# Key and query products in two halves, and new order lists for all engines, in a gated mix of two attention layers

## The chip, the core and the metric

The kernel runs on one core of a Trainium2 chip. The time is the device time of one execution in microseconds (us). Before the change the median of three runs is 811.47 us (808.78 to 812.91).

## What is computed

Two attention layers run on the same input `x` (2048 rows of 512) and are mixed by a gate. `h` has 32 heads; layer A works in 64 segments of 32 rows, and each segment sees 8 memory rows, which are an output of the segment before it. That makes a chain of 64 links.

```python
g = _sigmoid((x * gate_w).sum(-1, keepdims=True))
return g * _A_ref(...) + (1 - g) * _B_ref(...)

# A: for each segment s of 32 rows
h = jnp.concatenate([mem, xs], axis=1)            # 8 + 32 rows
q, k, v = (jnp.einsum('btd,dhe->bhte', h, W) for W in (Wq, Wk, Wv))   # 32 heads of 128
p = _softmax(jnp.where(mask, jnp.einsum('bhqe,bhke->bhqk', q, k) * scale, -1e9))
o = jnp.einsum('bhte,hed->btd', jnp.einsum('bhqk,bhke->bhqe', p, v), Wo)
mem = o[:, :M, :]                                 # goes into the next segment
outs.append(o[:, M:, :])

# B: four blocks of 512 rows, 32 heads of 16: causal softmax inside a block, plus a
# linear-attention memory (phi(k)^T v) of the blocks before, mixed by sigmoid(beta), then wo
```

## The kernel before

**How the work is tiled.** For each segment of layer A TensorE (PE) makes the products of 32 rows (24 of the segment and the 8 memory rows, tile `hT`) with Wk, Wq and Wv. The 32 rows are the loaded weights, in four column groups of the array at once; the big matrices stream through in chunks of 512 columns. The contraction over 512 goes in four chunks. A product of one half of the heads (`r` is 0 or 1) has 4 chunks of 4 matmuls. `wproj` issues it. The products of the last 8 rows of each segment do not depend on the memory; they are made for four segments at a time (tile `xr`, names beginning with `r`, function `p_rest`), the value part goes out to memory (`rest_v`) and comes back (`rem_v`).

The names and lines used below:

- `k`, `q`, `v`: products of a segment, line 1466 (with a weight load) and line 124 (function `again`: the weights that are still in the array are used once more). The query product of the second half of the heads is made in two column halves of 256.
- copies out of PSUM by ACT or DVE: line 1040 (`st`, `V_sb`, `OT_sb`); transposes of keys and queries by DVE: line 1544.
- scores `S` (lines 1559, 1563), their exp on ACT (1568), sums `U` (1586, 124), logarithm and reciprocal on ACT (1589, 1591), normalisation on DVE (1593) and on DVE or GpSimd (1595).
- `PV` and `PW` (lines 1626, 1635): probabilities times values, row-tiled.
- output product `wo` (line 1352), turned by DVE (1370), swapped (1374) and added (1377): this gives the memory rows in `hT` for the next segment.
- layer B: logits (1184), exp (1202), mask on GpSimd (1208), values (1225), projections (1067, 1069); it fills the gaps of layer A. Changing between column-tiled, row-tiled and full use of the array is a change of mode.

**What sets the order.** Every operation is created once with its engine or a choice of engines, what it reads and writes, and a cost. The text `ORDER` holds, packed, one list of operation numbers for each of the five engines; `sequences` unpacks it, and `schedule` follows it (`given`). So the order on every engine, and the engine of each operation that has a choice, are what the text says. The planner's constants (`LATENCY`, `TO_PE`, the instruction packets of 256 in `fetched`) give each operation a time; with the order fixed, these times only choose PSUM banks and which waits are written out. 

**Weights that are held.** Operations of one `Share` may take their chunks in any order. `turn` walks along the TensorE order; an operation that directly follows one with the same key begins with the chunk whose weights are in the array, without a load:

```python
c = held[1] if held and held[0] == key and held[1] in left else left[0]
o.plan.append((c, held != (key, c), len(left) == o.share.total, len(left) == 1))
```

From segment 1 on, `k` and `q` products were one operation of four chunks, `v` products four operations of one chunk (argument `n` of `wproj`).

Of the kernel before, what the change touches and what calls it, by code (L numbers as in the profile page):

```python
# [15 lines left out]
    "c-nPY2Vhji)1STeF4uA?v>=^?&|5%yhY+L$k)VQrAcWpkgiu0n(u)*9k<bOC_Z~XZi6|=kK|vr1sdu@%x9^*MS6(^31g`Acot^TV-^^~-M`r8XMp|Ig6oFooTVNYGXX@;)^wVtFn%O{L-i3n@*B#C`"  # L16
    "cT8)`LDw(V+82JAtt+I@qaW7dJ+F6O<rWX!RP=Jz<srAqWx$1DtA>?2_3if0W`@qlw5DbQY`7VjYwVpKQ)%I}LVoT<LJ8;GqD_E^HxQonL(&U?D!)}Z7!SLWTI$>Y`$7ugVO=9QjPTkF@LQGo06jhD"
    "&Q3Ym!9(@~!1dJ0nwXEtthlv}Yv|lJp+VC#zq_F3L-=~*fA|>6Xh}2vQj3=*&viP~>T>O<pIcsQ05@`Mjp1%BfO83ln}0VFZl8rF=_!Q(99wdt9qcs~m_GUek_jPtx7o=#PoGH*b!d1EK+VT#Jz+=6"
    "%sy=PxfW~ztO2<4e)@5K?MQRBz1}H(c-0FQPazm_`ZIvaZa6aHwO=~g1P1FTL~G41=E~KYxJ&@EM+^5M&JDi;v?>5FdM6%*0+YQXuhp6z#<%u@Fjt-^a>GbBoc<ba0T{gV;LDw;Qpx5QU*TNdhC4y1"
    "tN9t6+H`(9H^jj_NR+m(p7wC5XFWhSo^uo5WIzSpz<bY1Km~Xnm<eTI;m)h59<L{8*i#(Hw_;S>`2btSFG@zwCG>thRTBM2_dVVBKy!Za1VSu0Y}Pq7kUQ!7{E_IQ<T({3)0(B=%euRwzF$s<5H2gE"  # L20
    "&;*OdgUJosf1fFt)((cPy4vtD3Cqztv=-g<xE!1dM(s6-Go5V$%bQ+=asK_MrlQ99Q|U3TCwg0ck=0pf*Fi3v=n;LlCcr%={xrl(;&%_hIKs`BBuxKW@7AFjXA<3c7Wlo~6M!0Sn9ss+O|lT-7XvrU"
    "e-kaQMGKq215}3K15@$}82&mE)=J*{14=b4Lj3$wt<YNRaadM}1_hgpo1i;bVACg(5~~;DO9hW3kDyqa1I+oMPQ-Q>OCId&3C@gIC@u#@e*Fs(Q+Ykw##Df$W7(XDOtfvSy^kcee!poeC-QpqvC#pG"
    "rs^C}xCmf=E}Owg)2jZ-c7KUbCzf@+0qoAgABO<$y%NT-c^q^&hBF?;K*`GMT0M@-vY8z?)$yR(vl`jYAR54}Gr+BSTVgYkVa;c#=$au+ZaIJ)Tj@+uf#$bd1WgFN6H^aiTkDU?4*^wyul>%NG#kD#"
    "o^1)R6Ya{zIOm`q4#&}MnmV_bU58-xF-haQ%`UV!2OXKlm>JW)h7d!xiD_)`>We=u&qA?R#Ts10k5<$mG|wwC8}sKkh(U?Fa>p)C4#Wy|g_wRD`YvYLipb3mojvZ`3Fy?RFd1USXa@FQ3k|Mq7#P=`"
    "C6M0u!7ki66oC%y(&znh78YIm_lg99Ut#hr_!v<@Y*Fw}6uf?8%{3K_TbpNb+4Egy*m{1egsu-^?!?cd+v^>AKC?;@v^&{$U%1=Tb{}HlTHZr+95}`fhL#c-j$s<)W$Yw`<8o}dwgRv>ypV6yusoWs"
    "`w}+&H$~EVJUHN|f!h#b=#94f?L`G)PLgNIv+?Fa-T<!TCGei4O5C=U(6CK|<88FzZyBZ3x?^`%hTFAYq8njv5^RS_|AWsq`^}6MU+oT}%`tOtN;}YTI`^kPYGDQ2*$wOTqb1pxRF#~w`G_3m>w_PF"
    "(Glttb7*a%9llSL(ZsRqaR8aq_=vnsy^FoJ^Lp;(xx`FU0Yo~?9w;<GKBF(6jR!gd4BrSkcPXt^^U{oT@mEQtplrsj%Nn<E!vZ)6kT6NkZ$7p#xg#?5T5$e2f)uVB6uMv}d0u)+3IkM{;Zwg0A5?=?"
    "Ee2}V!h>&ktw?Y!&Y5{bwi(e<8<4=|Nj3i~06vo;B*Il_DzN4vMpI$cFqrE{X}c3Rulaen1GjqAEA>pzbH-d<D9Hj_k?0IJ6kYp3bQ*#ge@cpiO^8rdH(tkJ-7t1N0MH3eyWw75$_>eFQz7ONq+{wu"
    "zIE7hb%^^LO~5Dg`%>NfYEGOBgIb=oL)I}~8=6Bb?HW#kFb5Ps<J(q0OZZ)NXx8R<v?esiR*28+XtY~*=p#2EjWr%C*<BtM<F_*8KZF_Qwm4X7WI$QK>^Rl=Ks+3QsAdun((u2bS6M>-tYpozpy0pj"
    "X2D;v@DOs}x45AYE^Ro(LL368+ThgVvnIn}eAi*(M`W@zg`3T_&blj_gQ+6YZw92LzLcaF2PiU>ex)tq%-NiAauoDKZHxvtEc<58$nFWlkl+rU1Xwi5r+Xx{#jiGAuXnpcfkD`#)jE%MGGC9)I6WHX"  # L30
    "#bePG4gL8;eEG%!+;{yBC+-W&vA;na?}GliOz?92vNd<$34@m8m??XQm&dnpFGVWQLACU77C<dj1^CMiuh?uUfUyHN0EE95IoVsG8Ns)|=!UHuZUCFd${Ax9=z{4}Ak}?LB)!X=uOsl{+x3#bM!OzV"
    "YsKpuU1T6*)M~<#pKZ^Ma>MSXRV1GchTSI<`G{<+L`Fx*hEI?&McgbJ1xw+<4oP5r#-{nanad_N5n(29!_5Y8wUryTMRk!R{!)~@i4J8Ptl@LD5SE1yX2t4pS#(j4-Ah+UKB~bg#^Cu)_h5Q;IV(;!"
    "=d+H-l-=xt3G$o5-;x5DwJ`RjuMUHKL+?UX0yuEgg@2^oBVfIAEUPJAyRlM&=fiz04?f2}=ZYk53N*w{XTRiehnO&R9=Tz|cu8K^k3CFA^bfjQH({aHp>yl9080H^2D`mLuGE|`cS2GHFGpDaC?4i4"
    "0LBppu(&|yof3lo!`Z^}e*@IM9p%2qYE?D69w3`VF&!cs9D+7D&$j>=ThxZKd#Ih}L3>K<SeAEmq2wp12>hVbsof6r$OC>IjiK34mXgJ=Xv}=z>leHLzDhjR6<*b_e0JB(C=HnvXp8erwsnBYXJ{u("
    "$rkr$vwX822#r}Yl;qloCB(^b;EDbpE1z`0roM;QjaW7*1d2Tk1&<NuS@s!V$WNnki$j)ChfqS0SoT23Cx}DK+mhf21$PKRqrckAyNuo;HZATR3bas7d7k5KA>x?(--?Gjfwc#^zMP)8?a!jYQCJd}"
    "vt3Ft7osj%IFS4!j#zuq+YIVoEg!y;ZBi4fGMF_Mh}80S)CR{qA%xm!J2+WY|JL%jydAfx{kN#${!eHm6eD^|Rurlo>e1>o)EdWHIW{S6sHk&jB}`DecTdq&>&hp`SzFffD)WhZdw(1|*n9JG-U3CI"
    "5OGIi!)vf{bSO3&SvIZLcX>vPu!V$)coIkEkNs|phT0xhix!PS4J;baqu<K+-T8t>X??O{p5i3h23l>`+C}$<dVNtky<<KN#g$?h^Nb9(AJZchSiizn@){ODONA#BPKZ5>H-gpv!ZA%bo@;fS*l@^$"
    "L1=y*HM>2DK6zFFnJC2TZai2}>xTnA*gu>#ANIf~>US&;Qpv5l_O}H6+x$+x*+WA#DXG@sTd0}s)Ha<t%cCu{u~>{<T2>?@uLqf)q~t%gIId{Sa-Id(i<hI_7!c-vy?e^^lz_I({ZFftZFCwT{`DNo"
    "l=82JrP17qyjL+a)qSCTndkIFI9VMVFrTS~VQBx&dn5056BAE#Q}hEAY58U1+|RYd=5-v$Mu7bKQI{if#8{$Hcy3}k+HFPs?lvIs{{89Eba^palv_O8E`}Lhw1rMV;q5N^tV89j2Vex}btHqciO~78"
# [1657 lines left out]
```

## Time and profile before

| | |
|---|---|
| median of three runs | 811.47 us (808.78 to 812.91) |
| profiled execution, its own time | 809.81 us |
| its span, first to last instruction | 808.1 us |
| PE (matmul) busy | 788.1 us, 98%, 23542 matmuls |
| PEld (weight loads) busy | 466.1 us, 58%, 21898 loads |
| DVE, ACT, GpSimd busy | 609.9, 560.4, 249.1 us |
| granted TensorE clock | 1.00 |

All durations come from the one profiled execution. A matmul is drawn from its start to a modelled end, and neighbours overlap, so a share of 98% does not mean that the columns of the array stream 98% of the time. In a row of the timeline stand the start, the duration, engine, line, operation and tiles, the count, and in brackets the idle time of the engine before it with what ended it. In a row of groups stand busy time, mean ns of one, and idle time before. In a row of stages stand the window, its length, then busy time and count of PE, PEld, DVE, ACT and GpSimd, the clock and the DMA share. In a row of waits stand the total, the number and the longest. "Issue" as a releaser means that the profile shows nothing that the engine waited for.

### The profile page before, as it was taken

Reading aid. Unit: us, or ns where it says so; the run is one execution under the profiler, and the core shown is the slowest. Engines: PE = TensorE matmul, PEld = TensorE weight load, DVE = VectorE, ACT = ScalarE, POOL = GpSimd, SP = SyncE. Lnnn points to the kernel's source line nnn. Section 1 sums busy time; section 2 is a strip of 40 time slices with the busy share of each in tenths; the row PEclk is TensorE's granted clock in tenths of the full one; section 3 lists DMA queues with packets and bytes.
Section 4 is the critical chain, followed back from the end, with each engine's and each line's share of the span. In section 5 each row is a group of like instructions: output and inputs, shape, how many; then the busy total and the mean of one; then the engine's idle time right before and its main releaser. Section 6 shows DMA issues by size and latency. Waiting matters only on the chain.

```text
span 808.1 us, 50000 instructions
## 1 busy us (share of the span) xinstructions
PE 788.1 (98%) x23542; PEld 466.1 (58%) x21898; DVE 609.9 (75%) x1578; ACT 560.4 (69%) x1322; POOL 249.1 (31%) x543
## 2 busy tenths in 40 slices
PE   9989999999999999999999999999999999999997
PEld 4445656656565566555567565565655655556655
DVE  4868776878888777777666777788867788776876
ACT  3676676676766766767777687676677776767773
POOL 3533231232332323431323331433323313323340
PEclk9999999999999999999999999999999999999999
DMA  8992112211111210111011211111020100000011
GB/s 314 417 273 45 44 30 50 44 30 30 46 31 28 41 34 20 45 35 46 20 35 40 46 44 17 33 29 26 28 59 23 43 24 16 11 26 16 17 35 36
DMA packets 71689, 45.02 MB, mean 56 GB/s; under 512 B 50046, under 2 KB 69942, under 8 KB 69942
## 3 DMA queue, kind: packets, MB, share of 16 engines
q1 hardware_dynamic: 70422, 40.92, 18.1%
q8 instruction: 178, 2.92, 1.5%
q10 hardware_dynamic: 1056, 0.92, 0.4%
q14 instruction: 33, 0.27, 0.1%
HBM read 30.33 MB, written 8.87 MB: 49 GB/s over the span
## 4 chain that ended last, share of the span: by engine, by line
PE 88%; DVE 5%; ACT 3%; DMA 1%; issue 1%; POOL 1%; SPq 0%; DVEq 0%; POOLq 0%
PE pb L1466 42%; PE pb L1352 18%; PE pb L124 6%; PE pb L1067 6%; PE pb L1184 4%; PE pb L1069 3%; PE pb L1225 2%; PE pb L1626 2%; PE pb L1559 1%; DMA rest_v<-stg 1%; PE pb L1586 1%; PE pb L827 1%; PE pb L1635 1%; PE pb L1563 1%; PE pb L1273 1%
## 5 line engine op out<-in xcount | busy, mean ns | idle before, releaser
L1040 ACT ACTIVATE st<-pb 128x512 bf16<-128x512 f32 (+2 forms) x291 | 135.3, 489 | 78.7 <-PE pb L1466 68.6
L1202 ACT ACTIVATE PTB<-pb 128x640 bf16<-128x640 f32 x240 | 157.6, 706 | 27.2 <-PE pb L1184 25.1
L1466 PE MATMUL pb<-Wv_sb,hT 128*32 128x512 bf16 x1760 | 139.0, 380 | 0.0
L1352 PE MATMUL pb<-Wo_sb,OT_sb 128*32 128x256 bf16 x4096 | 134.2, 274 | 3.1 <-issue 1.9
L1466 PE MATMUL pb<-Wq_sb,hT 128*32 128x256 bf16 (+1 forms) x2604 | 129.8, 311 | 1.0 <-DVE hT L1377 0.6
L1466 PE MATMUL pb<-Wk_sb,hT 128*32 128x512 bf16 x1716 | 116.5, 379 | 0.2
L1352 PEld LDWEIGHTS pb<-Wo_sb,OT_sb 128*32 128x32 bf16 x4096 | 99.4, 96 | 19.5 <-ACT OT_sb L1040 2.8
L1208 POOL TENSOR_SCALAR_AFFINE_SELECT PTB<-PTB 128x512 bf16<-128x512 bf16 x120 | 78.0, 650 | 98.2 <-ACT PTB L1202 92.8
L1466 PEld LDWEIGHTS pb<-Wq_sb,hT 128*32 128x32 bf16 x2604 | 67.5, 97 | 58.1 <-issue 32.4
L1040 ACT ACTIVATE OT_sb<-pb 128x320 bf16<-128x320 f32 (+2 forms) x162 | 65.7, 426 | 46.2 <-PE pb L1635 45.5
L1466 PEld LDWEIGHTS pb<-Wk_sb,hT 128*32 128x32 bf16 x1716 | 45.8, 97 | 53.3 <-issue 17.5
L1544 DVE STREAM_TRANSPOSE QT_sb<-st 128x128 f32<-128x128 f32 (+1 forms) x192 | 62.5, 336 | 17.3 <-ACT st L1040 15.3
L1595 POOL TENSOR_TENSOR PT_sb<-PT_sb,rc_sb 128x64 bf16<-128x64 bf16 x68 | 25.8, 379 | 155.3 <-ACT rc_sb L1591 154.1
L1544 DVE STREAM_TRANSPOSE KT_sb<-st 128x256 f32<-128x256 f32 x128 | 55.3, 432 | 18.2 <-ACT st L1040 16.5
L1040 DVE CAST V_sb<-pb 128x512 bf16<-128x512 f32 x82 | 56.1, 685 | 14.9 <-PE pb L1466 14.0
L1589 ACT ACTIVATE rc_sb<-pb 128x160 f32<-128x160 f32 x128 | 38.8, 303 | 36.3 <-PE pb L124 36.0
L1370 DVE STREAM_TRANSPOSE pb<-pb 128x256 f32<-128x256 f32 x63 | 29.3, 465 | 44.8 <-PE pb L1352 44.4
L1040 DVE CAST OT_sb<-pb 128x320 bf16<-128x320 f32 x98 | 47.1, 481 | 19.2 <-PE pb L1635 18.3
L1466 PEld LDWEIGHTS pb<-Wv_sb,hT 128*32 128x32 bf16 x1760 | 43.6, 98 | 24.4 <-issue 4.3
L1517 POOL COPY QT_sb<-rem_q 128x256 bf16<-128x256 bf16 x64 | 28.9, 452 | 89.9 <-PE pb L1563 63.0
L1593 DVE TENSOR_TENSOR PT_sb<-PT_sb,rc_sb 128x160 bf16<-128x160 bf16 x128 | 43.8, 342 | 14.4 <-ACT rc_sb L1591 13.1
L1568 ACT ACTIVATE PT_sb<-pb 128x224 bf16<-128x224 f32 x128 | 45.3, 355 | 12.4 <-PE pb L1563 7.9
(211 smaller groups left out, 1576.6 us busy)
## 6 DMA issues: line engine op xcount, KB each, us to landing
Wv_sb<-in_A_Wv_dram SPq DMA_DIRECT2D x4, 1024.0 KB, 10.9
Wk_sb<-in_A_Wk_dram SPq DMA_DIRECT2D x4, 1024.0 KB, 20.3
Wq_sb<-in_A_Wq_dram SPq DMA_DIRECT2D x4, 1024.0 KB, 27.5
Wo_sb<-in_A_Wo_dram SPq DMA_DIRECT2D x4, 1024.0 KB, 21.1
rest_v<-stg SPq DMA_DIRECT2D x112, 32.0 KB
rem_v<-rest_v SPq DMA_DIRECT2D x28, 128.0 KB, 2.3
a_rows<-ao SPq DMA_DIRECT2D x63, 32.0 KB
stg<-a_rows SPq DMA_DIRECT2D x15, 128.0 KB
```

What stands on the lines that cost most here:

```text
L124: return pe.add_instruction(mybir.InstMatmult(name=pe.bass.get_next_instruction_name(), start_tensor_calc=start, stop_tensor_calc=stop, in ...
L1040: self.P.op(("act", "dve"), (lambda a: a.activation(dst, src(), ACT.Copy), lambda d: d.tensor_copy(dst, src())), reads=reads, writes=write ...
L1067: ins = pe.matmul(out[32 * c:32 * c + 32], lhsT[:, 32 * c:32 * c + 32], rhs, start=start, stop=stop, tile_position=(0, 32 * c), **kw)
L1184: ins = pe.matmul(pb[slot.banks[i]][:, base + a - lo:base + b - lo], KT[r0:r1, 128 * kc:128 * kc + 128], Q[r0:r1, t0 + a:t0 + b], start=Tr ...
L1202: P.op("act", (lambda dst=dst, src=src: lambda a: a.activation(dst, src(), ACT.Exp, scale=0.25))(), reads=[pair], writes=["%s%d_%d" % (nam ...
L1208: P.op("gp", (lambda pt=pt, ii=ii: (lambda g: g.affine_select(pt, pt, ([[0, len(ii)]] if len(ii) > 1 else []) + [[1, 128]], ALU.is_ge, 0.0 ...
L1352: ins = pe.matmul(pb[so.b][p0:p0 + 32, 0:256], tok(r, g, l), half(h, d, q), start=(r == 0 and g == 0 and l < 2), stop=(r == 1 and g == 3 a ...
L1466: ins = pe.matmul(out, own, part[:, g], start=start, stop=stop, tile_position=(0, 32 * g))
L1544: op("dve", (lambda dst=dst, src=src: lambda d: d.transpose(dst, src))(), reads=["st%d%s" % (i, tag)], writes=["%sT%d%s" % (kind, r, tag)] ...
L1568: op("act", lambda a: a.activation(PT[:, r, :], pb[rb.b][:, 0:224], ACT.Exp, scale=SCALE), reads=[rb], writes=["PT%d" % r, "PT%dr" % r], n ...
L1589: op("act", lambda a: a.activation(rc[:, r, :], pb[rb.b][:, 0:160], ACT.Ln), reads=[rb], writes=[rr], name="ln%d_%d" % (s, r), cost=0.325, ...
L1593: op("dve", lambda d: d.tensor_tensor(mine[r], mine[r], by_head(rc[:, r, :]), ALU.mult), reads=[rp, rr], writes=[rp], name="nrm%d_%d" % (s ...
```

## The change

Four things change.

1. `k` and `q` products of segments 1 to 63 are two operations of two chunks each; products of the first segment and `v` stay.
2. The planner's constants: hand-overs from PE, ACT, DVE and GpSimd are longer, and an instruction packet is asked for 0.9 us after the one before it has been reached, not sooner than 3.9 us after the last asking, and arrives 2.5 us later. Before, two packets were simply kept 3.55 us apart.
3. The planner's `load` of the stores to `rest_v` goes from 0.1 to 0.25.
4. `ORDER` is replaced: a new order for all five engines, and with it another choice of engine for operations that have one. It must be another one, since 315 operations are new.

```diff
 ORDER = (
-    "c-nPY2Vhji)1STeF4uA?v>=^?&|5%yhY+L$k)VQrAcWpkgiu0n(u)*9k<bOC_Z~XZi6|=kK|vr1sdu@%x9^*MS6(^31g`Acot^TV...
+    "c-nPY31Cdu*FX2ozGX5I60yWqwJSyJr4%K0YN@@d8iJyzqWGh=G*P0qYPCr0gjhoDyINYRReP;PWH*^)-rV<{``*mFCHY1&X6`%p...
...
-    LATENCY = {"pe": 0.235, "act": 0.05, "dve": 0.05, "gp": 0.1, "sp": 2.0}
-    TO_PE = {"pe": 0.0, "act": 0.04, "dve": 0.04, "gp": 0.08, "sp": 0.0}
+    LATENCY = {"pe": 0.25, "act": 0.06, "dve": 0.06, "gp": 0.13, "sp": 2.0}
+    TO_PE = {"pe": 0.0, "act": 0.05, "dve": 0.05, "gp": 0.1, "sp": 0.0}
...
-    FETCH = 3.55
+    FETCH = 3.9
+    ASKED = 0.9
+    ARRIVES = 2.5
...
-                if tb < last + wait:
-                    late += last + wait - tb
-                    tb = last + wait
-                last = tb
+                if tb < last + self.ARRIVES:
+                    late += last + self.ARRIVES - tb
+                    tb = last + self.ARRIVES
+                last = max(tb + self.ASKED, last + wait)
...
-                          name="rvst%d_%d_%d" % (j, r, l), prio=prio + 0.001 * l, load=0.1, cost=0.4)
+                          name="rvst%d_%d_%d" % (j, r, l), prio=prio + 0.001 * l, load=0.25, cost=0.4)
...
-                self.wproj(rb, kind, r, hv, [rx, rm], "%s%d_%d%s" % (kind, s, r, tag), prio, 4 if kind == "v" or s == 0 else 1,
+                self.wproj(rb, kind, r, hv, [rx, rm], "%s%d_%d%s" % (kind, s, r, tag), prio, 4 if kind == "v" or s == 0 else 2,
```

More of the change, by code (lines that the diff above doesn't have):

```diff
@@ L20 @@
[L20 to L27, printed above, removed]
```

112 lines of the change are left out of this document (61 added, 51 removed).

## The prediction

> **What bounds the kernel now.** I read the page first: span, busy times, the chain of waits, the queues.
>
> ```profile
> span 808.1 us, 50000 instructions
> ...
> PE 788.1 (98%) x23542; PEld 466.1 (58%) x21898; DVE 609.9 (75%) x1578; ACT 560.4 (69%) x1322; POOL 249.1 (31%) x543
> ...
> q8 instruction: 178, 2.92, 1.5%
> ...
> PE 88%; DVE 5%; ACT 3%; DMA 1%; issue 1%; POOL 1%; SPq 0%; DVEq 0%; POOLq 0%
> ```
>
> TensorE sets the time; no other engine is above 75%. An order of work can therefore win only the time in which TensorE's columns stand still. The busy time by stage shows how much of that is visible:
>
> ```profile
> 0.00:60.00 60.00, 55.56 (x986) 27.29 (x978) 38.18 (x101) 34.32 (x69) 26.45 (x72) 1.00 0.95 338
> 60.00:780.00 720.00, 709.62 (x21868) 424.94 (x20280) 551.84 (x1429) 514.05 (x1219) 218.73 (x463) 1.00 0.14 33
> 780.00:808.10 28.10, 22.92 (x700) 13.88 (x644) 19.87 (x49) 11.99 (x36) 3.95 (x9) 1.00 0.10 29
> ```
>
> PE is idle 4.4 us in the head (60 - 55.56), where the DMA share is 0.95, 10.4 us in the 720 us of the segments, and 5.2 us in the last 28 us. The clock is 1.00 throughout. Busy is not streaming, though, and the timeline tells by how much:
>
> ```profile
> 400.27 0.21 PE L1563 MATMUL pb<-QT_sb,rem_k 128*32 128x64 bf16 x4
> ...
> 400.58 0.36 ACT L1568 ACTIVATE PT_sb<-pb 128x224 bf16<-128x224 f32 x1 [0.16 <-PE pb L1563]
> ...
> 401.76 0.46 DVE L1544 STREAM_TRANSPOSE QT_sb<-st 128x128 f32<-128x128 f32 x2
> ...
> 402.27 0.17 PEld L1559 LDWEIGHTS pb<-QT_sb,KT_sb 128*32 128x32 bf16 x16 [0.61 <-DVE QT_sb L1544]
> ...
> 403.60 0.61 PE L1067 MATMUL pb<-xT,wkB_sb 128*32 128x512 bf16 x8
> ...
> 404.14 0.27 PE L1626 MATMUL pb<-PT_sb,V_sb 32*128 32x40 bf16 x16
> ...
> 409.04 1.04 PE L1466 MATMUL pb<-Wk_sb,hT 128*32 128x512 bf16 x16
> ...
> 409.91 0.39 PE L124 MATMUL pb<-Wq_sb,hT 128*32 128x512 bf16 x4
> ...
> 410.12 0.82 PE L1466 MATMUL pb<-Wq_sb,hT 128*32 128x512 bf16 x12
> ...
> 410.77 0.28 PE L124 MATMUL pb<-Wq_sb,hT 128*32 128x256 bf16 x4
> ```
>
> Four things stand here. The key product, 16 matmuls with 16 weight loads, starts at 409.04 and the next product at 409.91: 0.87 us, or 0.217 per chunk of four. Each matmul is drawn 0.39 long, so a stop of up to 0.17 us stays invisible. The query product behind it has only 12 loads, the first four matmuls (L124) using weights still held, and takes 0.86 (409.91 to 410.77): a spared load is worth 0.01 at most. A change of array mode: eight matmuls from 403.60 should free the columns at 404.03, the row-tiled L1626 starts at 404.14, so 0.11 us. A hand-over: the scores end at 400.48 as drawn, their exp starts at 400.58; with the invisible 0.17 that is 0.27 from the last column, and the way back from DVE to PE (402.22 to 402.27) is 0.05.
>
> **The change, part by part.** The order lists are text in the diff. Unpacked, each is a list of operation numbers for one engine, and they can be counted against the operations that the code creates. The numbers in this part that have no row are such counts.
>
> *Two halves.* 63 segments have five key and query products each (k of both halves of the heads, q of the first, q of the second in two column halves). Each becomes two operations of two chunks: 2971 TensorE operations become 3286. Columns streamed do not change. 195 of the 315 pairs stay back to back; in 120 something is put between, mostly halves of other products (172), then masks (27), scores (22) and v chunks (18). Held weights are met more often: matmuls with loads go from 21898 to 21680, 218 loads fewer. Matmuls grow by 30, because ten that ran on the full array now run in column mode in four parts. Loads lie under the matmuls (466 us of PEld under 788 of PE), price by the row above at most 54 x 0.01 = 0.5 us, taken as 0. A half alone needs a due moment only 0.43 us long instead of 0.87.
>
> *Mode changes* go from 390 to 385: 5 x 0.11 = **-0.6 us**.
>
> *Who copies.* ACT goes from 1327 to 1311 operations, DVE from 1578 to 1597, GpSimd from 539 to 536; mainly swaps of the memory rows move from ACT to DVE. DVE gains 19 x about 0.3 = 6 us and stands at 76%: no term while it has 24% left. SP keeps 367 transfers in a new order; the only stop that one of its transfers causes on PE is 1.3 us, below, taken as it is.
>
> *Hand-overs.* What can now be late is a TensorE operation whose operand comes back from another engine. The links and their lengths:
>
> ```profile
> L1040 ACT ACTIVATE OT_sb<-pb 128x320 bf16<-128x320 f32 x155 | 64.1, 433 | 45.6 <-PE pb L1635 45.1
> ...
> L1040 DVE CAST OT_sb<-pb 128x320 bf16<-128x320 f32 x97 | 46.7, 483 | 19.2 <-PE pb L1635 18.3
> ...
> L1593 DVE TENSOR_TENSOR PT_sb<-PT_sb,rc_sb 128x160 bf16<-128x160 bf16 x128 | 43.8, 342 | 14.4 <-ACT rc_sb L1591 13.1
> ...
> L1591 ACT ACTIVATE rc_sb<-rc_sb 128x160 f32<-128x160 f32 x128 | 42.9, 335 | 3.0
> ...
> L1589 ACT ACTIVATE rc_sb<-pb 128x160 f32<-128x160 f32 x128 | 38.8, 303 | 36.3 <-PE pb L124 36.0
> ...
> L1370 DVE STREAM_TRANSPOSE pb<-pb 128x256 f32<-128x256 f32 x63 | 29.3, 465 | 44.8 <-PE pb L1352 44.4
> ...
> L1595 POOL TENSOR_TENSOR PT_sb<-PT_sb,rc_sb 128x64 bf16<-128x64 bf16 x68 | 25.8, 379 | 155.3 <-ACT rc_sb L1591 154.1
> ...
> L1377 DVE TENSOR_TENSOR hT<-pb,other_sb 128x32 bf16<-128x32 f32 x63 | 12.0, 190 | 7.7 <-ACT other_sb L1374 3.8
> ...
> L1374 ACT ACTIVATE other_sb<-pb 64x32 f32<-64x32 f32 x62 | 11.8, 191 | 21.1 <-DVE pb L1370 18.8
> ```
>
> So from the sums U to the values PV: 0.303 + 0.335 + 0.342 and the hand-overs, 1.3 us; from PV to the output product: 0.43 or 0.48; from the output product to the next segment's k and q: 0.465 + 0.19 + 0.19. Against each I set the work that the TensorE order puts in between (0.217 per chunk, 0.11 per mode change). Waits in the engines' own queues are left out, so this is a lower bound of what is missing. In the old order 68 such places lack cover, 19.3 us together: 0.9 in the head, 10.7 in segments 2 to 60, 7.7 in the last three. That is of the size of the visible idle (20.0 us). In the new order 67 places lack 20.3 us: 1.2, 12.9 and 6.2. The last three segments gain 1.5 us, but the memory rows' way into k and q (L1377 to L1466) lacks 3.5 instead of 2.1, and PV and PW 5.9 instead of 5.1. Term: **+1.0 us**; bounds -10.7 (all of the middle covered) and +10.7 (as much again lost where queues delay an operand).
>
> *Longer hand-overs.* The planner now counts 0.25 instead of 0.235 from PE, 0.06 instead of 0.05 from ACT or DVE and 0.05 instead of 0.04 into PE. The rows above show 0.27 from PE: the new figures are nearer to them, and an order made with them keeps operands apart by 0.015 + 2 x 0.01 to 0.015 + 3 x 0.01, so up to 0.045 us more per passage. At 68 places, 68 x 0.045 = 3.1. Bounds 0 and -3.1; I take the whole, **-3.1 us**, since the gap between 0.235 and 0.27 is of that size.
>
> *Instruction packets.* TensorE's 45440 instructions come in 178 packets (q8), 256 each; the new order needs 45252. The planner now lets a packet arrive 2.5 us after it was asked for, with 3.9 between two askings. In the trace, stops of PE with no releaser are the candidates:
>
> ```profile
> PE pb L1352 <- issue: 2.3, 3, 1.4
> PE pb L1466 <- DMA rest_v<-stg: 1.3, 2, 0.9
> ...
> PE pb L1067 <- issue: 1.0, 3, 0.4
> ```
> ```profile
> 252.73 0.39 PE L1352 MATMUL pb<-Wo_sb,OTr_sb 128*32 128x256 bf16 x8
> 253.58 0.40 PE L1352 MATMUL pb<-Wo_sb,OTr_sb 128*32 128x256 bf16 x8 [0.45 <-issue]
> ```
>
> The output product stops there in its middle, with all operands there. Of the 3.3 us, 1.4 is one stop, long for a packet; 1.9 are left. Bounds: all gone, -1.9, or as much again, +1.9. I take half of the gain, **-0.95 us**, since such stops sit in the middle of dense work that a denser order would repeat. A rule of the Trainium skill speaks against this term (Runtime: NRT & Kernel Launch, Instruction fetch mechanics): instructions are fetched ahead in blocks of 256, and crossing into the next costs one bump of a queue, mostly hidden. The trace agrees on the block (2.92 MB in 178 packets) and, with few visible stops in 178, on "mostly"; by the page the term is 0 and the sum would be 0.95 higher.
>
> **Sum.** -0.6 + 1.0 - 3.1 - 0.95 = -3.65 us. The profiled execution took 809.81 us (span 808.1 and 1.7 around it), so 806.2 for such a one. The median of the runs, 811.47, lies 1.66 above it: **807.8 us**, 0.45% faster.
>
> **Rivals.** *The cover really is there* (800 us). If the margins also absorb the queues, the 10.7 us missing in the middle go and the last segments keep their 1.5: 809.81 - 10.7 - 1.5 + 1.66 = 799.3, say 800. For it: the visible idle and the missing cover are of one size, so there is that much to win. Against: the new order, counted in the same way, lacks as much.
>
> *Halves that finish late* (slower, 818 us). Where 172 halves of other products lie between the two of one, both products end together; each then reaches its copy on ACT and its transpose on DVE 0.43 us later than alone, and two copies queue. Scores wait for these transposes:
>
> ```profile
> PEld pb L1559 <- DVE QT_sb L1544: 5.2, 17, 0.7
> ...
> PEld pb L1559 <- DVE KT_sb L1544: 3.5, 12, 0.6
> ```
>
> If one in four of the 120 split products is the last that a score waits for, 30 x 0.43 = 12.9 us, less some 0.2 of cover each: 7 us; 809.81 + 7 + 1.66 = 818. It decides once these two rows rise from 8.7 to above 15 us. Against: 195 pairs stay whole, and today's order too ran k and q products in pairs that end close together.
>
> *Nothing reaches the chip* (811.5 us, within 1.5). A planner's constant is no instruction; with the columns unchanged and 68 against 67 bare places, stops may only change place. Against: the order is another one on every engine, so exact balance would be chance.
>
> **How the numbers follow.** Forecast, 804 to 811: 0.45, of which 0.20 lies below 807.4 (0.5% under 811.47, which is about what a measurement of this kernel can tell from no change) and 0.25 above. The cover is there: 0.20, faster. Late halves: 0.22, of which 0.19 above 815.5. Nothing: 0.13, nearly all within. Faster 0.20 + 0.20 = 0.40; slower 0.19 and 0.01 of the rest, 0.20; same 0.40. The range runs from 799, which cuts off the better half of the first rival, to 817, which cuts off the worse half of the second: under 0.2 outside. The likeliest one's own range is 804 to 811.
>
> **What would show it.** PE x23572, PEld x21680, DVE x1597 and 177 packets show that I counted the order rightly. PE's idle between 60 and 780 should fall from 10.4 to about 8 us and in the last 28 us from 5.2 to about 4. The rows PE <- issue should fall below 3.3 us. The waits of k and q for hT (L1377) should rise a little, those of L1559 for QT and KT stay near 8.7 us. The prediction is wrong if idle in the middle rises with L1559's waits (late halves), if ACT or DVE operands come late at places where the order has cover, so that queues and not cover decide, or if the last segments grow.

## The result, and the profile after

The changed kernel takes 813.51 us (median of 11 runs, 811.85 to 817.19). The kernel before, on the same chip, takes 808.91 (11 runs, 806.06 to 812.91). The ratio is 1.0058, 95% interval 1.0036 to 1.0080: slower by 0.6%, or 4.7 us. Forecast was 807.8 where the kernel before had 811.47, so 0.45% faster. The time lies in the stated range, but the direction was wrong, so that says nothing for the account.

The page of the profile after, span, busy times, instruction queue and chain of waits:

```profile
span 813.2 us, 49863 instructions
...
PE 789.5 (97%) x23572; PEld 455.9 (56%) x21680; DVE 609.6 (75%) x1597; ACT 562.3 (69%) x1306; POOL 245.4 (30%) x540
...
q8 instruction: 178, 2.92, 1.5%
...
PE 88%; DVE 5%; DMA 2%; ACT 2%; issue 1%; SPq 1%; POOL 0%; DVEq 0%; POOLq 0%
```

Matmuls, loads and DVE operations are those that were counted from the lists. PE is busy 1.4 us longer as drawn (789.5 against 788.1), and the rest of the 5.1 us by which the span grew is idle time. Where, the busy times by stage tell (stretch, its length, then busy time of PE, PEld, DVE, ACT, GpSimd, clock, DMA share):

```profile
0.00:60.00 60.00, 55.59 (x991) 27.17 (x983) 38.88 (x104) 34.44 (x68) 26.56 (x73) 1.00 0.94 338
60.00:780.00 720.00, 707.07 (x21769) 412.87 (x19945) 549.01 (x1443) 512.18 (x1197) 210.11 (x450) 1.00 0.14 33
780.00:813.30 33.30, 26.84 (x828) 15.90 (x756) 21.69 (x53) 15.67 (x42) 8.77 (x19) 1.00 0.13 38
```

PE's idle time is 4.4 us in the head as before, 12.9 in the middle (10.4 before) and 6.5 behind 780 us (5.2 before; the last stretch holds 128 matmuls more, since the work arrives there later). The waits of PE after (waiting line, what released it, total us, times, longest):

```profile
PE pb L1356 <- issue: 2.1, 4, 0.7
PE pb L1639 <- DMA rem_v<-rest_v: 1.6, 1, 1.6
PE pb L1356 <- ACT OT_sb L1044: 1.5, 3, 0.7
PE pb L1188 <- DVE PT_sb L1597: 1.3, 3, 0.5
PE pb L831 <- DVE phiK L825: 1.2, 1, 1.2
PE pb L1470 <- DVE hT L1381: 1.2, 5, 0.3
...
PE pb L1071 <- issue: 0.9, 2, 0.7
...
PE pb L1188 <- issue: 0.8, 2, 0.6
```

Line numbers are four higher than before (L1356 is the output product, L1352 before). Three things differ. Stops without a releaser ("issue") add up to 4.7 us, with 0.6 on L1470 and 0.3 on L126 that are not shown; before they were 3.3. The product on old value rows (`PW`, L1639) stands 1.6 us for its load, which it did not before; the stop of 1.3 us for `rest_v<-stg` is gone in return. And the memory rows' way into k and q (`hT`) costs 1.2 us instead of 0.6. The waits of the weight loads:

```profile
PEld pb L1470 <- DVE hT L1381: 9.6, 27, 0.6
...
PEld pb L1563 <- DVE QT_sb L1548: 5.3, 21, 0.5
PEld pb L1563 <- DVE KT_sb L1548: 2.2, 8, 0.4
```

Before, the two rows of `hT` were these:

```profile
PE pb L1466 <- DVE hT L1377: 0.6, 2, 0.4
```
```profile
PEld pb L1466 <- DVE hT L1377: 6.7, 22, 0.6
```

`hT` rises, as was forecast; the scores' waits for the turned queries and keys fall from 8.7 to 7.5.

None of these rises is as large as the loss; the issue rows rise by 1.4 us. The experiments show that what stands behind the issue rows, the places where instruction packets end, can move the time by as much as the loss.

### The profile page after: what moved, and what is told of

Read it like the earlier page. It is cut to its first block, busy times and chain, and to the rows that moved or that the text cites. A ratio compares the mean times of both kernels' runs of the same rounds, so it can differ in the third digit from the quotient of the medians.

```text
span 813.2 us, 49863 instructions
## 1 busy us (share of the span) xinstructions
PE 789.5 (97%) x23572; PEld 455.9 (56%) x21680; DVE 609.6 (75%) x1597; ACT 562.3 (69%) x1306; POOL 245.4 (30%) x540
## 4 chain that ended last, share of the span: by engine, by line
PE 88%; DVE 5%; DMA 2%; ACT 2%; issue 1%; SPq 1%; POOL 0%; DVEq 0%; POOLq 0%
PE pb L1470 42%; PE pb L1356 17%; PE pb L126 8%; PE pb L1071 6%; PE pb L1188 4%; PE pb L1630 2%; PE pb L1229 2%; PE pb L1073 2%; PE pb L1563 2%; DMA Wv_sb<-in_A_Wv_dram 1%; PE pb L1590 1%; PE pb L1639 1%; PE pb L1277 1%; PE pb L1567 1%; DVE PT_sb L1597 1%
## 5 line engine op out<-in xcount | busy, mean ns | idle before, releaser
L1044 ACT ACTIVATE st<-pb 128x512 bf16<-128x512 f32 (+2 forms) x290 | 138.1, 496 | 83.2 <-PE pb L1470 71.2
L1356 PE MATMUL pb<-Wo_sb,OT_sb 128*32 128x256 bf16 x4096 | 134.0, 274 | 4.2 <-issue 2.1
L1470 PE MATMUL pb<-Wq_sb,hT 128*32 128x256 bf16 (+1 forms) x2468 | 134.1, 313 | 1.5 <-DVE hT L1381 1.0
L1470 PE MATMUL pb<-Wv_sb,hT 128*32 128x512 bf16 x1720 | 133.4, 380 | 0.0
L1470 PE MATMUL pb<-Wk_sb,hT 128*32 128x512 bf16 x1632 | 117.2, 379 | 0.3 <-DVE hT L1381 0.2
L1356 PEld LDWEIGHTS pb<-Wo_sb,OT_sb 128*32 128x32 bf16 x4096 | 100.1, 96 | 19.8 <-issue 4.3
L1470 PEld LDWEIGHTS pb<-Wq_sb,hT 128*32 128x32 bf16 x2468 | 61.7, 97 | 65.6 <-issue 38.3
L1044 ACT ACTIVATE OT_sb<-pb 128x320 bf16<-128x320 f32 (+1 forms) x154 | 62.8, 428 | 43.8 <-PE pb L1639 42.5
L1599 POOL TENSOR_TENSOR PT_sb<-PT_sb,rc_sb 128x64 bf16<-128x64 bf16 x61 | 22.1, 362 | 168.1 <-ACT rc_sb L1595 167.4
L1470 PEld LDWEIGHTS pb<-Wk_sb,hT 128*32 128x32 bf16 x1632 | 41.9, 97 | 53.7 <-issue 22.1
L1044 DVE CAST V_sb<-pb 128x512 bf16<-128x512 f32 x82 | 56.1, 684 | 11.8 <-PE pb L1470 11.2
L1044 DVE CAST OT_sb<-pb 128x320 bf16<-128x320 f32 (+1 forms) x106 | 50.2, 478 | 19.2 <-PE pb L1639 17.9
L1470 PEld LDWEIGHTS pb<-Wv_sb,hT 128*32 128x32 bf16 x1720 | 41.0, 98 | 27.3 <-issue 6.4
L1597 DVE TENSOR_TENSOR PT_sb<-PT_sb,rc_sb 128x160 bf16<-128x160 bf16 x128 | 45.2, 353 | 10.2 <-ACT rc_sb L1595 9.3
L1044 ACT ACTIVATE stg<-pb 128x512 bf16<-128x512 f32 (+1 forms) x75 | 42.2, 564 | 12.4 <-PE pb L1470 9.2
```

The source lines that it names most:

```text
L1044: self.P.op(("act", "dve"), (lambda a: a.activation(dst, src(), ACT.Copy), lambda d: d.tensor_copy(dst, src())), reads=reads, writes=write ...
L1356: ins = pe.matmul(pb[so.b][p0:p0 + 32, 0:256], tok(r, g, l), half(h, d, q), start=(r == 0 and g == 0 and l < 2), stop=(r == 1 and g == 3 a ...
L1470: ins = pe.matmul(out, own, part[:, g], start=start, stop=stop, tile_position=(0, 32 * g))
L1597: op("dve", lambda d: d.tensor_tensor(mine[r], mine[r], by_head(rc[:, r, :]), ALU.mult), reads=[rp, rr], writes=[rp], name="nrm%d_%d" % (s ...
```

## The experiments

### Is it the order, the halves or the constants?

First the parts of the change one at a time; each diff is against the changed kernel. The lists of all engines as before, with each product of keys and queries as two neighbouring halves and with the new constants:

```diff
 ORDER = (
-    "c-nPY31Cdu*FX2ozGX5I60yWqwJSyJr4%K0YN@@d8iJyzqWGh=...
+    "c-nn=2S8Lu*Y=say|FA{EU^c%qEWGHh@zl^7$bH~?7b(N7)yc$jrC...
```

> The halves and the new constants, but the old order on every engine, the two halves of a product directly behind each other. By count TensorE's instructions are those of the kernel before (23542 matmuls, 21898 loads); only PSUM banks and written-out waits can differ. Theory A (the new order itself lost time): ratio to the kernel before 1.000, within 0.003. Theory B (the new constants' choice of banks and waits lost it): 1.006.

Measured: 1.0009 (0.9997 to 1.0021), span 807.1. Halves and constants by themselves cost 0.7 us (0.0009 x 809), between -0.2 and 1.7. The two halves of a product stay together here; halves with something between them exist only in the new order.

The new order with the old constants (and the old spacing of packets and load of stores in the planner), which then only decide banks and waits:

```diff
-    LATENCY = {"pe": 0.25, "act": 0.06, "dve": 0.06, "gp": 0.13, "sp": 2.0}
-    TO_PE = {"pe": 0.0, "act": 0.05, "dve": 0.05, "gp": 0.1, "sp": 0.0}
+    LATENCY = {"pe": 0.235, "act": 0.05, "dve": 0.05, "gp": 0.1, "sp": 2.0}
+    TO_PE = {"pe": 0.0, "act": 0.04, "dve": 0.04, "gp": 0.08, "sp": 0.0}
...
-    FETCH = 3.9
-    ASKED = 0.9
-    ARRIVES = 2.5
+    FETCH = 3.55
```

> The new order on every engine, with the planner's constants of the kernel before (hand-overs, packets, load of the stores). Theory A (the order): 1.006 to the kernel before, as the changed kernel. Theory B (the constants): back to 1.000.

Measured: 1.0048 (1.0032 to 1.0064). So the loss comes with the lists.

### Which part of the order?

Both kernels' lists cut at the output product of segment 33 and joined: new lists first, then old; and old first, then new.

```diff
 ORDER = (
-    "c-nPY31Cdu*FX2ozGX5I60yWqwJSyJr4%K0YN@@d8iJyzqWGh=...
+    "c-nPa2VfM%*MGCuTP~LbLJu_pQUpVl(4__t2vS6fqF?|CNL4_<fKp...
```
```diff
 ORDER = (
-    "c-nPY31Cdu*FX2ozGX5I60yWqwJSyJr4%K0YN@@d8iJyzqWGh=...
+    "c-nPa2Vhgx*FX1Vucj$QhHTkWHpo&ov`~<OOl7Y^K~O}dWy@6d5{i...
```

> The new order up to the output product of segment 33, the old order from there on. In the two profiles the changed kernel is 3.5 us behind at the end of segment 24, level at segment 33 and 5 us behind at the end. If these differences belong to the order (theory A): ratio 1.000 to 1.001. If each profile's course is chance and the loss is spread evenly (theory C): 1.003.

> The old order up to the output product of segment 33, the new order from there on. Theory A, from the two profiles: all of the 5 us is lost behind segment 33, ratio 1.006. Theory C (spread evenly): 1.003.

Measured: 1.0036 (1.0018 to 1.0053) and 1.0016 (1.0004 to 1.0027). The two add up to nearly the whole, but the loss is not behind segment 33, where two profiles had put most of it. A third cut followed what the profiles seemed to say next: segments 26 to 33 gained time in the new order, so they alone were taken from it.

```diff
 ORDER = (
-    "c-nPY31Cdu*FX2ozGX5I60yWqwJSyJr4%K0YN@@d8iJyzqWGh=...
+    "c-nn>2S8KT_y4&sdl3S(j*6>@+g8QB>cRnHt+TE=>z=Jv>!>(z(`w...
```

> Old order on every engine up to segment 25, the new order from there to segment 33, the old order to the end; halves and constants as in the changed kernel. Beside the old order, the new one lost time up to segment 25 and won 1.6 to 3.4 us back in segments 26 to 33 (three profiles). Theory 'gain and loss have their own places': the stretch keeps its gain without the loss ahead of it, ratio 0.9968 (0.9955 to 0.9985), 1.3 to 3.6 us under the kernel before. Rival 'won back only because it had been lost' (the engines behind TensorE had run ahead in the delay): 1.000 (0.999 to 1.0015).

Measured: 1.0038 (1.0024 to 1.0052). Both theories fall: a stretch that had gained in three profiles makes the kernel slower when it stands in the old order. At this point "which part of the order" was no longer a sensible question; the next runs say why.

### Where the instruction packets fall

In the trace after, four long stops without a releaser stand in output products and masks: at 244.4, 315.1, 539.1 and 705.2 us, 0.90, 0.83, 0.59 and 0.81 us from the estimated end of the columns' work (the views draw them 0.1 to 0.2 shorter, because a matmul is drawn longer than it streams). A fifth stands in layer B's logits at 611.4 us, drawn 0.59:

```profile
611.37 0.31 PE L1188 MATMUL pb<-QTm,KT 32*128 32x320 bf16 x3 [0.59 <-issue]
```

TensorE's instructions come in packets of 256. To move the packets and nothing else, the warming products (operations named `warm`) at the very start were cut into smaller ones: the same columns, more instructions ahead of everything, so that each later packet begins earlier in the work. The bank plan was held still by counting these products as before.

```diff
-                    o.i[m] = c.i + self.EXTRA.get(o.name.rstrip("0123456789_b"), 0.0)
+                    o.i[m] = (2 if o.mode == "full" and o.name[:4] == "warm" else c.i) + self.EXTRA.get(o.name.rstrip("0123456789_b"), 0.0)
...
-                return pe.matmul(pb[sw.b][:, 0:512], self.phiK[:, 0, :], self.phiQ, start=True, stop=True)
+                for j in range(0, 512, 128):
+                    last = pe.matmul(pb[sw.b][:, j:j + 128], self.phiK[:, 0, :], self.phiQ[:, j:j + 128], start=True, stop=True)
+                return last
```

> New order; the 23 warming products on phiK at the start are each cut into four of a quarter of the columns: 69 products and 69 weight loads more ahead of everything, the same columns. That shifts what each instruction packet holds by 138 of 256 instructions, and nothing else. In the changed kernel single stops without a releaser stand at 244.4 (0.90 us), 315.1 (0.83), 539.1 (0.59) and 705.2 us (0.81). Theory 'packets': these four go, and stops of 0.3 to 0.9 us come at other lines, each with an instruction packet begun 2.2 to 2.9 us ahead of it; the time changes by up to 2 us either way, likelier down, ratio 1.004 (1.002 to 1.0065). Rival 'these stops belong to the work' (a bank, the product itself): they stay with the same products, and the ratio stays at 1.0058.

There are 24 such products, not 23, so the shift is 24 x 3 x 2 = 144 instructions. Measured: 0.9989 (0.9976 to 1.0003). The same order, 144 instructions later, is 0.7% or 5.6 us faster, and no longer slower than the kernel before. The four stops are gone, and others stand at other products.

> The kernel before with the same 23 warming products cut into four: 69 products and 69 loads more at the start, the old order. Theory 'packets': its stops without a releaser at 253.6 (0.57 us), 135.7 (0.49), 358.8 (0.49) and 420.4 us (0.41) move elsewhere; the time within 1 us of before, ratio 1.000 (0.9985 to 1.0015). Rival: they stay at the same products.

Measured: 1.0053 (1.0037 to 1.0069). The same edit makes the old order as slow as the changed kernel. None of the four old stops named is left at its product; the longest are now drawn 1.2, 1.1 and 1.0 us, at other products. Neither change of time had been expected to that size. Shifts by 64 and by 192 instructions follow, for both orders, with products cut into 2, 4 or 8:

```diff
-            def f_warm(pe, sw=sw):
+            def f_warm(pe, sw=sw, cut=(4 if i < 5 else 2 if i < 22 else 1)):
```
```diff
-            def f_warm(pe, sw=sw):
+            def f_warm(pe, sw=sw, cut=(8 if i < 8 else 4 if i < 21 else 2 if i < 22 else 1)):
```

> New order; the warming products at the start are cut so that 64 instructions (products and loads) more stand ahead of everything, the same columns: a quarter of an instruction packet. Measured so far: shift 0 gives 1.0058, shift 144 (24 products cut into four) 0.9989; with the old order shift 0 is 1, shift 144 gives 1.0053. Theory 'where the packets fall': the time depends on the shift by some tenths of a per cent in both orders, and the mean over shifts 0, 64, 144 and 192 is the same for both orders within 0.002; this one anywhere from 0.998 to 1.006. Rival 'the new order is slower by itself and shift 144 is a lucky one': 1.004 to 1.007 here and at shift 192.

> New order, 192 instructions more ahead of everything (three quarters of a packet), the same columns. Theory 'where the packets fall': 0.998 to 1.006, and the mean of the four shifts within 0.002 of the old order's mean. Rival 'slower by itself': 1.004 to 1.007.

> The kernel before with 64 instructions more at the start, the same columns. Theory 'where the packets fall': 1.000 to 1.006 and not the same as shift 0 at all shifts; the mean of the four shifts 1.002 to 1.003. Rival 'the old order is indifferent, shift 144 was an unlucky one': within 0.0015 of 1 here and at shift 192.

> The kernel before with 192 instructions more at the start, the same columns. Theory 'where the packets fall': 1.000 to 1.006; the four shifts together average 1.002 to 1.003. Rival 'the old order is indifferent': within 0.0015 of 1.

Another start could itself be the cause: the head's course, or what follows from it. A shift by a whole packet tells. It changes the start the most, and leaves each packet with the instructions that it had:

```diff
-            def f_warm(pe, sw=sw):
+            def f_warm(pe, sw=sw, cut=(8 if i < 14 else 4)):
...
-                return pe.matmul(pb[sw.b][:, 0:512], self.phiK[:, 0, :], self.phiQ, start=True, stop=True)
+                for j in range(0, 512, 512 // cut):
+                    last = pe.matmul(pb[sw.b][:, j:j + 512 // cut], self.phiK[:, 0, :], self.phiQ[:, j:j + 512 // cut], start=True, stop=True)
+                return last
```

> New order with 256 instructions more at the start, the same columns: the start is changed the most of all shifts, but the packets hold the same instructions as in the changed kernel, one packet later. Theory 'where the packets fall': back at the changed kernel's time, 1.0058 (1.004 to 1.0075), with single stops without a releaser at the same products as there (near 244, 315, 539 and 705 us, at least two of the four over 0.5 us). Rival 'what the cut products change at the start decides' (the head's course, the clock's steps): as shifts 144 and 192 or better, 0.998 to 1.002.

> The kernel before with 256 instructions more at the start, a whole packet, the same columns. Theory 'where the packets fall': as the kernel before, 1.000 (0.9985 to 1.002), though shifts of 144 and 192 gave 1.0053 and 1.0036. Rival 'the longer start costs the old order time': the more instructions the slower, 1.004 to 1.007.

Measured, ratios to the kernel before with their intervals:

| shift, instructions | old order | new order |
|---|---|---|
| 0 | 1 | 1.0058 (1.0036 to 1.0080) |
| 64 | 1.0007 (0.9991 to 1.0022) | 1.0053 (1.0036 to 1.0071) |
| 144 | 1.0053 (1.0037 to 1.0069) | 0.9989 (0.9976 to 1.0003) |
| 192 | 1.0036 (1.0020 to 1.0053) | 1.0003 (0.9988 to 1.0019) |
| 256 | 1.0011 (0.9999 to 1.0024) | 1.0042 (1.0026 to 1.0057) |
| mean of 0 to 192 | 1.0024 | 1.0026 |

Both orders return after 256 to where they were, within the intervals: it is the packets' places and not the start. And averaged over four places the two orders take the same time. Each interval is about 0.0016 to either side, a mean of four 0.0008, the difference of two means 0.0011; so 0.0002 is 0.2 us, give or take 0.9. That covers the measurement alone. How well four placings stand for all others is less certain: by the spread of the ratios within each column, the difference of the two means has a standard error of about 0.002, or 1.7 us.

The timeline shows it at one product. In the kernels with cut warming products line numbers are two higher again (L1358 is the output product). TensorE around the mask product of 244 us, in the changed kernel (start, duration, line, operation, count, idle time before it):

```profile
242.72 0.83 PE L1356 MATMUL pb<-Wo_sb,OT_sb 128*32 128x256 bf16 x24
243.38 0.24 PE L1071 MATMUL pb<-hide_sb,neg_sb 128*32 128x160 bf16 x2
244.35 0.25 PE L1071 MATMUL pb<-hide_sb,neg_sb 128*32 128x160 bf16 x2 [0.74 <-issue]
```

With a shift of 256:

```profile
242.40 0.24 PE L1073 MATMUL pb<-hide_sb,neg_sb 128*32 128x160 bf16 x2
243.37 0.25 PE L1073 MATMUL pb<-hide_sb,neg_sb 128*32 128x160 bf16 x2 [0.74 <-issue]
```

With a shift of 144:

```profile
242.22 1.27 PE L1358 MATMUL pb<-Wo_sb,OT_sb 128*32 128x256 bf16 x40
243.31 0.24 PE L1073 MATMUL pb<-hide_sb,neg_sb 128*32 128x160 bf16 x4
243.38 0.72 PE L1358 MATMUL pb<-Wo_sb,OTr_sb 128*32 128x256 bf16 x20
```

After a whole packet the stop is back in the middle of the same four matmuls, 0.74 us long as before; at 144 the four run through and the output product starts 0.07 us behind them. That the length is the same is luck: the new order with the old constants, with the same TensorE list, stops one matmul later for 0.29 us, and the version with earlier loads below, also with the same TensorE list, not at all. Of the other long stops, those of 539 and 705 us are back after 256 (0.62 and 0.39 us), that of 315 is not. So the packet fixes where TensorE can stop, but whether and how long it stops there changes between profiles. For 705 us, the changed kernel, then shift 256, then shift 144, where the output product of 32 matmuls runs through:

```profile
705.21 0.40 PE L1356 MATMUL pb<-Wo_sb,OT_sb 128*32 128x256 bf16 x6 [0.66 <-issue]
```
```profile
702.80 0.40 PE L1358 MATMUL pb<-Wo_sb,OT_sb 128*32 128x256 bf16 x6 [0.39 <-issue]
```
```profile
699.48 1.06 PE L1358 MATMUL pb<-Wo_sb,OT_sb 128*32 128x256 bf16 x32
700.36 0.39 PE L1472 MATMUL pb<-Wv_sb,xr 128*32 128x512 bf16 x4
```

A stop also moves by as much as the packets do. Near 420 us the version with earlier loads (shift 0) stops inside a mask product, the new order at a shift of 64 inside a projection of layer B, and at 144 inside the output product ahead of it:

```profile
420.70 0.25 PE L1071 MATMUL pb<-hide_sb,neg_sb 128*32 128x160 bf16 x3 [0.40 <-issue]
```
```profile
419.98 0.40 PE L1073 MATMUL pb<-wvB_sb,xT 128*32 128x128 bf16 x15 [1.07 <-issue]
```
```profile
418.82 0.62 PE L1358 MATMUL pb<-Wo_sb,OT_sb 128*32 128x256 bf16 x16 [0.75 <-issue]
```

Counted from the end of the program these are the 11622nd, 11654th and 11694th matmul: 32 and 72 matmuls earlier in the work, which with their weight loads are the 64 and 144 instructions.

How the 5.2 us between the spans of shift 0 and shift 144 build up (end of the 64 matmuls of a segment's output product in both traces, us):

| behind segment | 1 | 7 | 9 | 10 | 15 | 16 | 20 | 21 | 29 | 30 | 39 | 40 | 46 | 47 | 53 | 54 | 63 |
|---|---|---|---|---|---|---|---|---|---|---|---|---|---|---|---|---|---|
| shift 0 | 74.7 | 146.5 | 170.0 | 183.1 | 243.6 | 256.0 | 302.6 | 315.4 | 409.1 | 421.0 | 528.0 | 540.0 | 609.8 | 623.1 | 692.7 | 706.7 | 808.9 |
| shift 144 | 75.8 | 146.0 | 171.1 | 182.9 | 243.5 | 255.1 | 301.5 | 313.4 | 406.8 | 419.7 | 526.4 | 537.6 | 607.1 | 619.5 | 689.0 | 701.6 | 803.7 |
| difference | -1.1 | 0.5 | -1.1 | 0.2 | 0.1 | 0.9 | 1.1 | 2.0 | 2.3 | 1.3 | 1.6 | 2.4 | 2.7 | 3.6 | 3.7 | 5.1 | 5.2 |

The difference grows and shrinks in steps. (In the head shift 144 has a stop of 1.2 us at 57.8 us, made up again by segment 7.) The segments of the five long stops of shift 0 (16, 21, 40, 47, 54) bring 0.8, 0.9, 0.8, 0.9 and 1.4 us, 4.8 together. The stops of shift 144 take some back: 1.6 in segments 8 and 9 (drawn 0.39 and 0.63) and 1.0 in segment 30 (0.75). So the stops of both explain 2.2 of the 5.2, and the issue rows, 4.7 against 3.7, only 1.0. The load of segment 10 brings 1.3, and the rest is waits for operands at other places; that these change with the placing is seen, why they do is not shown.

### Is the late load a cost of its own?

In the changed kernel two loads into `rem_v` stand in SP's list behind a row of stores and other loads. They were put ahead of them; the list around the two, by the names of the transfers:

```diff
 rlv2_1
+rlv2_0
 dma_x1_3
...
 rvst2_0_2
-rlv2_0
 rvst3_0_2
...
 ain1
+rlv10
 rvst4_1_2
 ast9
 rvst4_1_1
 rvst4_1_0
-rlv10
 dma_out1
```

> New order; only SyncE's list differs from the changed kernel: two loads of old value rows into rem_v (segments 2 and 10) are put ahead of the row of stores and loads behind which they were issued. In the changed kernel the products on these rows stood 1.6 us for the load in one profile and 2.8 us in two places in the profile with the old constants; the old order has no such wait. Theory 'late loads': the row L1639 <- DMA rem_v<-rest_v leaves the PE waits and the time falls by 1.6 to 2.8 us, ratio to the kernel before 1.003 (1.001 to 1.0042) instead of 1.0058. Rival 'something else is late there anyway' (the probabilities or the state that the same products need come as late): the row is gone, the time stays, 1.005 to 1.0065.

Measured: 1.0027 (1.0012 to 1.0042), and the row L1639 <- DMA is gone, as the theory of late loads had it. But another placing alone can do as much, so the same list was run at three shifts, with the cuts shown above, and at one between the best two:

```diff
-            def f_warm(pe, sw=sw):
+            def f_warm(pe, sw=sw, cut=(8 if i < 3 else 4)):
```

> New order with the two loads into rem_v put earlier, and 64 instructions more at the start. With one placing of the packets the earlier loads gave 1.0027 instead of 1.0058, which is less than a shift of the packets can do. Theory 'late loads cost 1.6 to 2.8 us whatever the packets do': each of the shifts 64, 144 and 192 lies 0.002 to 0.0035 under the new order's at the same shift (1.0053, 0.9989, 1.0003), here 1.002 to 1.0035, and the mean of the four shifts is 0.9995 (0.999 to 1.0006) instead of 1.0026. Rival 'it was the placing of the packets': the mean of four is 1.002 to 1.003.

> New order with the two loads put earlier, and 144 instructions more at the start. Theory 'late loads': 0.9964 (0.995 to 0.998), under both kernels. Rival 'placing': 0.998 to 1.001.

> New order with the two loads put earlier, and 192 instructions more at the start. Theory 'late loads': 0.9975 (0.996 to 0.999). Rival 'placing': 0.999 to 1.002.

> New order with the two loads into rem_v put earlier and 168 instructions more at the start, between the two shifts that gave the shortest times. If the time changes smoothly with the places of the packets: 0.9985 (0.997 to 0.9995), just under the kernel before. If single packets decide: anywhere from 0.996 to 1.003.

Measured: 1.0052 (1.0035 to 1.0070), 0.9995 (0.9984 to 1.0006), 0.9986 (0.9971 to 1.0000) and, at 168, 1.0027 (1.0013 to 1.0040). The mean over shifts 0, 64, 144 and 192 is 1.0015, against 1.0026 with the late loads: 0.9 us better, give or take 0.9. A gain of 1.6 to 2.8 us at every placing is not there (at 64 and 144 there is none); whether a smaller one is, these runs can't tell. The profiles show one reason: the late load itself depends on the placing. In the new order without the earlier loads its row is 1.6 us at shift 0, 1.4 at 256 and 0.5 at 64, and at 144 and 192 it is not there though the list is the same. The time does not change smoothly either: 168 lies between two fast shifts and is not fast.

No version beats both kernels for certain. The nearest are this one at a shift of 192 and the plain new order at 144, both with intervals that reach 1.

### What the profiles of all these kernels have in common

The issue rows of PE in the changed kernel with earlier loads, and in the same at a shift of 144:

```profile
PE pb L1356 <- issue: 3.4, 5, 1.2
...
PE pb L1470 <- issue: 0.8, 2, 0.7
PE pb L1188 <- issue: 0.7, 2, 0.4
...
PE pb L126 <- issue: 0.6, 1, 0.6
...
PE pb L1071 <- issue: 0.4, 1, 0.4
```
```profile
PE pb L1190 <- issue: 1.1, 1, 1.1
...
PE pb L1472 <- issue: 0.3, 1, 0.3
...
PE pb L1073 <- issue: 0.2, 1, 0.2
```

5.9 against 1.6 us, spans 811.8 and 805.2. Summed in this way for each kernel:

| order, shift | span | issue | DMA | other waits |
|---|---|---|---|---|
| old, 0 | 808.1 | 3.3 | 1.3 | 9.9 |
| old, 64 | 806.5 | 1.7 | 1.1 | 10.2 |
| old, 144 | 811.6 | 4.5 | 2.2 | 10.3 |
| old, 192 | 810.6 | 2.7 | 1.7 | 10.7 |
| old, 256 | 805.3 | 2.2 | 1.3 | 9.7 |
| new, 0 | 813.2 | 4.7 | 2.1 | 11.6 |
| new, 64 | 810.2 | 3.9 | 1.0 | 10.6 |
| new, 144 | 808.0 | 3.7 | 0.6 | 10.2 |
| new, 192 | 806.8 | 2.5 | 0 | 11.3 |
| new, 256 | 810.6 | 3.9 | 1.4 | 11.2 |
| earlier loads, 0 | 811.8 | 5.9 | 0 | 10.8 |
| earlier loads, 64 | 814.3 | 6.6 | 1.1 | 10.3 |
| earlier loads, 144 | 805.2 | 1.6 | 0.2 | 10.1 |
| earlier loads, 168 | 811.6 | 5.7 | 0.9 | 11.3 |
| earlier loads, 192 | 806.1 | 2.4 | 1.1 | 10.1 |

With the five other kernels of this study added, the correlation of span and issue is 0.85 over 20 profiles, and a us of issue goes with 1.5 us of span. The waits for other engines stay between 9.7 and 11.6 whatever the order. But each profile is one execution, and one kernel's executions differ too (the changed kernel's by 5.3 us). The issue column correlates at 0.81 with how far the profiled execution lay from its own kernel's median, and at only 0.59 with the kernels' ratios. So the column carries a part of what separates the kernels, and not all: the old order at a shift of 192 is slow with only 2.7. What else such placings cost (stops too short to be drawn, or waits that follow from them) stays open.

That the issue stops are waits for instruction packets, the records of the instruction queue show. The 20 profiles have 112 such stops of 0.2 us or more. Of these, 108 end 2.1 to 3.0 us after the record of a packet began. Of all matmuls only 20% start in that stretch behind a packet, and of the stops put down to another engine or a DMA in four of the profiles 21 of 95 end there.

This also bears on the cut orders above. Old and new lists hold different numbers of weight loads, so a joint changes the packets behind it. Ratios of 1.0036, 1.0016 and 1.0038 lie within what a placing alone does to one order (0.9989 to 1.0058), and show nothing of segments.

## Why the prediction was wrong

*The counts* were right: matmuls, loads and DVE operations to the unit; 178 packets instead of 177.

*Two halves at nothing*: right as far as it was measured. With the old order, where they stay together, they give 1.0009 (0.9997 to 1.0021), at most 1.7 us.

*Mode changes, uncovered hand-overs and longer hand-overs*, together -0.6 + 1.0 - 3.1 = -2.7 us, are what the order does apart from the packets. Averaged over four placings that is +0.2 us, give or take 0.9 by measurement and with a standard error of 1.7 for the choice of placings. The term that failed here is the third. The waits of PE for other engines did not fall by 3.1: over five placings they are 10.2 us in the old order and 11.0 in the new one (means of the table). PE's idle time, as the length of the span less its busy time, is 20.3 us in the old order and 20.7 in the new one, as means of the profiles at shifts 0, 64, 144 and 192. The count of uncovered places, 67 that lack 20.3 us against 68 that lack 19.3, had been made on the finished list, so whatever the longer constants gained was in it already; to subtract 3.1 again was to count it twice. Without it the sum of these terms is +0.4, which agrees with these figures, but in part by luck, since the parts of the +1.0 did not come as counted. The middle was to lose 2.2 us: its idle time is 10.9 us in the old order and 11.3 in the new one, as means over the same four placings. The last three segments were to gain 1.5: from the end of segment 60's output product to that of segment 63's they take 36.9 us instead of 35.8, at four of five placings of each order, and PE's idle time from there to the end of the program is 6.6 us instead of 6.3. The mode changes by themselves were not measured.

*Instruction packets*, -0.95 us with bounds of 1.9 to either side: this step, too, failed, and it gave the wrong sign of the forecast: without the 3.1 alone the sum would still be -0.55. Against the mean of its placings, the new order at shift 0 lost 0.0032 x 809 = 2.6 us, the old one gained 0.0024 x 809 = 1.9: the term is +4.5 us, and with +0.2 for the order it is the 4.7 measured, as it must be, since both come out of the same ratios. The mistake was to price packets by the stops seen in one profile of one placing, as if they belonged to the kind of work. They belong to the one place where a packet ends. A changed list draws a new set of such places, so the term had no expected gain, and its bounds had to come from how far such a draw reaches: 5.6 us between two placings of the new order, 4.3 of the old. No view of one trace gives that; its rows gave 3.3 us of visible stops, and half of a part of that became a gain. The stop of 1.4 us that was set aside as long for a packet ends 2.55 us after a packet's record began, like the others.

*SP's new order at no term*: the old stop of 1.3 us went, one of 1.6 came. As a sum that was nearly right. Of SP's list only the place of two loads was tried by itself; by the runs at four placings that is worth at most about 2 us.

*The rivals.* "Halves that finish late" was to show in L1559's waits above 15 us; they fell to 7.5, so it is refuted by its own mark, although its sign came true. "The cover really is there" is refuted by the idle time in the middle, 12.9 us, where the old order has 10.4 and the rival would have left almost nothing; it is not below 10.2 at any of the new order's five placings. "Nothing reaches the chip" is the nearest to what the order does on the mean of placings: stops change place. Its own range of 1.5 us did not hold at this one. Whether the balance of the two orders is more than chance, four placings can't tell.

*What would show it.* Idle in the middle and at the end, and the issue rows, went the other way; `hT` rose as forecast, and the scores' waits, which were to stay near 8.7 us, fell a little. The last segments grew, which had been named as a sign of being wrong.

## What to carry to other kernels

Two versions of a kernel that is bound by TensorE's instruction stream, and whose lists differ, should not be ranked by one run each when they differ by half a per cent: shift both by 64, 128 and 192 instructions at the start, where that costs nothing, and compare the means (the runs here took 64, 144 and 192). If the means agree, the placing is a thing to choose by itself, last, since any later edit draws it anew. And a cost that was counted on the finished order already holds what the planner's constants did to it.

## What the chip showed that was not expected

- The place of a stop for instructions can be reproduced: after a shift of exactly 256 instructions it is back between the same two pairs of matmuls, and after shifts of 64 and 144 a stop stands 32 and 72 matmuls earlier in the work. Its length does not reproduce (0.74, 0.74, 0.29 and none at the mask product of 244 us, in four profiles with the same TensorE list at shift 0 or 256).
- In the records of the instruction queue, the four long stops of the changed kernel end 2.2 to 2.4 us after a packet's record begins, and that record begins 4.7 to 5.7 us behind the one ahead of it, later than the median of 4.3. They lie in dense work: output products and masks in four column parts. That TensorE waits for the packet is shown by the 108 of 112 stops and by their moving with the packets; that it is the density of the work that makes one packet late and another not fits these four and was not tried by itself.
- The Trainium skill (Runtime: NRT & Kernel Launch, Instruction fetch mechanics) says that crossing into the next block of 256 instructions is mostly hidden. Of 178 packets in the changed kernel at most eleven show as a drawn stop, by the counts of its issue rows (4, 2, 2, 2 and 1), so "mostly" agrees; but how the packets fall was worth 5.6 us of 809 between two placings of one order, and there the measurement decides.
